# Block-sparse attention feeding a top-1 mixture of experts: five routing groups, unscaled copies of K, early gathers freed from the later scatters, setup moved

## The chip, the cores and the metric

The kernel runs on one core of a Trainium2 chip. The metric is the time of one execution in device microseconds, as the median of three runs. The trace is of one execution of its own. Engines are named as in the profile: PE multiplies matrices, PEld loads its weights, DVE, ACT and POOL are the vector, scalar and GpSimd engines, SP issues direct DMAs. Each engine works through its instructions in the order in which they were written; an instruction that waits holds up everything behind it on the same engine.

## The reference

```python
scores = q @ k.T / sqrt(64)                 # batch 4, heads 8, 768 tokens, 24 blocks of 32
mask: neighbouring blocks, first and last block row and column, 3 sampled blocks per block row
attn = softmax(where(mask, scores, -1e9)) @ v          # -> x of 3072 rows x 512
e_idx = argmax(x @ w_gate)                             # 8 experts, one per row
gate = softmax(x @ w_gate)[e_idx] * sigmoid(x @ w_output_gate)[e_idx]
out = gate * (relu(x @ w1[e_idx]) @ w2[e_idx])         # 512 -> 1024 -> 512
```

All inputs are fp32. The sampled blocks and the routing are data, so K and V blocks are fetched by index at run time and rows of x travel through a table in DRAM that is sorted by expert.

## The kernel before

**Steps of the attention.** The work is written out as steps. Two batch pairs (bp 0 and 1) take 26 steps each: four dense ones for the first and last block row (`Dense`), then 22 sparse ones (`Sparse`): 11 pairs of block rows, each pair in two steps (head groups 0 and 1). Sparse steps of bp 0 are steps 4 to 25, of bp 1 steps 30 to 51. In a step PE writes the scores S (line 507, or 574 in a dense step), DVE takes the row maxima (514, 583), ACT the exponentials P (522, 591); one step later PE transposes P to T (471), ACT and DVE copy it to SBUF; two steps later PE multiplies it with V into O (539, 550, 608), and DVE normalises into a slot of the ring `xall` (483 to 485). S and T each have two PSUM buffers. The program text of step n is: S of n, hooks of rank 0, O of n-2, maxima of n, hooks of rank 1, normalisation of n-2, hooks of rank 2, T of n-1, exponentials of n, hooks of rank 3. Side work is hung on a step and a rank with `at(step, rank, ...)`.

**Feeding a sparse pair.** For pair i with first step u0, POOL copies six sampled blocks of K by index into one of three buffers `kr` (`gather_k`, line 439) at the ends of steps u0-3 and u0-2, DVE copies the four neighbouring blocks (`window_k`, 445 and 446), and POOL fetches the V rows with two indirect DMAs (`gather_v`, 456) in steps u0-1 and u0. Every copy of K multiplies by 1/8. The first and last K block are put into the three buffers once per bp (`fixed`, 415). q of a pair comes by DMA into a ring of four slots, `qall` (`load_q`, 405).

**Routing.** A tile is 128 rows of x; there are 24, twelve per bp. A finished tile is transposed (`turn`, 630; ACT's or DVE's copy to xT is 634 or 636) and multiplied with the gate weights (`route_p`, 646). Tiles are ranked in groups (`RG`): `route_a` (ten DVE instructions), `route_r` (PE products with a triangle and with ones, 689 to 694), `route_b` (two on ACT), `route_c` (seven or eight on DVE), then for each tile one scatter of its rows into the table `rows` in DRAM by POOL (`route_d`, 760), out of its slot of `xall` (tile t has slot t mod NX). All of a group's work hangs on the step in which its last tile is done.

**Early expert.** After group GE, that is after twelve tiles, the fullest expert is chosen (`choose`). 512 rows of it are gathered out of the table (`load_early`, 902, four gathers) and turned (`turn_early`, 913, 917, 918) while attention still runs, so that the experts can begin before all rows are placed. The framework orders an access of `rows` behind earlier ones that it can't tell apart; scatters are declared independent of each other, and the gathers name the scatters that they need.

**Experts.** Behind step 53 the program of the experts is dealt out (`program`): pieces n of 128 hidden columns, eight to a unit of rows. Per piece ACT and DVE split the fp32 weights into two fp16 parts (`w_h` 972, `w_l` 976), PE computes h (`p_h`, 998), ACT and DVE split h (`h_h` 1007, `h_l` 1013), PE computes y four pieces later (`p_y`, 1033). h takes the two PSUM buffers of T. Within a program step, work is sorted by rank. `plan` (0, 1, 2) computes on DVE, with one small product (831), where the remaining rows lie; the gathers of all later units wait for it.

**Start.** PE first runs 66 products on a tile of ones (`warm`), then the dense steps as their K, q and V land.

Of the kernel before, what the change touches and what calls it, by code (L numbers as in the profile page):

```python
# [33 lines left out]
NX = 8  # L34
# [28 lines left out]
RG = ((0, 3), (3, 6), (6, 9), (9, 12), (12, 16), (16, 19), (19, 22), (22, 24))  # L63
GT = max(b - a for a, b in RG)

GE = 3
# [22 lines left out]
XE = 52, 53  # L89
XG = 42, 43, 48, 49  # L90

LATE_T = 52
PARTS = (5, 5, 4), (6, 9)

KC = (("pool", 3, (0, 1, 2)), ("pool", 2, (3, 4, 5)))
NWARM = 66
WARM = {}
# [31 lines left out]
def tile_kernel(ctx, tc, q, k, v, sampled, wg, wcat, out):  # L129
# [39 lines left out]
    xs0 = const.tile([128, 2, 4, EU], F16, name="xs0")  # L169
# [11 lines left out]
    eighth = const.tile([128, 1], F32, name="eighth")  # L181
# [13 lines left out]
    nc.vector.memset(eighth, EXPS)  # L195
# [90 lines left out]
    def setup_vals():  # L286
        nc.vector.tensor_copy(pw, pl["places"])
        nc.vector.tensor_copy(stack[:, 1, 0:8], bins[0:PS])
        nc.vector.tensor_scalar(ckey, bins, -16.0 * LS - 1.0, 8.0, op0=ALU.mult, op1=ALU.add)
# [5 lines left out]
    def setup_index():  # L295
# [4 lines left out]

        vf = sp.tile([128, 2, 12], F32, name="vf")
# [109 lines left out]
    e8th = eighth.unsqueeze(2).to_broadcast([128, 4, 64])  # L411

    def fixed(bp, r):
        for j in range(2):
            nc.gpsimd.tensor_tensor(
                kr[r][:, 10 + j], kn[bp][:, :, 23 * j], e8th, op=ALU.mult)
# [7 lines left out]
    def gather_k(bp, i, kind, ns):  # L424
# [5 lines left out]
        for n, rv in zip(ns, regs):  # L430
            slot = n + 4 if n < 3 else n - 2
            if kind == "dve":
                nc.vector.tensor_single_scalar(
                    r[:, slot], kn[bp][:, :, ds(rv, 1)].rearrange("p u o n -> p u (o n)"), EXPS, op=ALU.mult)
            elif kind == "act":
                nc.scalar.activation(
                    r[:, slot], kn[bp][:, :, ds(rv, 1)].rearrange("p u o n -> p u (o n)"), AF.Copy, scale=EXPS)
            else:
                nc.gpsimd.tensor_tensor(  # L439
                    r[:, slot], kn[bp][:, :, ds(rv, 1)].rearrange("p u o n -> p u (o n)"), e8th, op=ALU.mult)  # L440

    def window_k(bp, i):
        a = 1 + 2 * i
        r = kr[i % RK]
        nc.vector.tensor_single_scalar(r[:, 0], kn[bp][:, :, a + 2], EXPS, op=ALU.mult)
        nc.vector.tensor_single_scalar(
            r[:, 7:10].rearrange("p s u n -> p u s n"), kn[bp][:, :, a - 1:a + 2], EXPS, op=ALU.mult)
# [309 lines left out]
    scattered = []  # L757

    def route_d(t):
# [5 lines left out]
        scattered.append(i.name)  # L765

# [133 lines left out]
    def gather_x(u, x, m):  # L900
        place_ = place_u[:, WALK[u - 1], m:m + 1] if u else place_0[:, m:m + 1]
        after_scatters(nc.gpsimd.indirect_dma_start(  # L902
            x.bitcast(I32), None, rows, bass.IndirectOffsetOnAxis(ap=place_, axis=0)).ins, NT if u else RG[GE][1])

# [201 lines left out]
    for bp in range(2):  # L1106
        o = PER * bp
        for r in range(RK):
            at(o + r, 3, fixed, bp, r)
# [244 lines left out]
```

## Time and profile before

| | us |
|---|---|
| median of three runs (533.68 to 539.52) | 534.85 |
| the profiled execution | 530.91 |
| its span in the trace, first to last instruction | 529.1 |
| PE busy | 494.4 |
| DVE, ACT, POOL busy | 360.6, 299.0, 259.2 |

Attention and routing take about the first 255 us, the experts run from about 245 us to the end. Start times in the timeline are microseconds from the start of the span. A bracket at the end of a line of the timeline is the idle time of that engine just before and what ended it.

### The profile page before, as it was taken

What the parts mean: (1) busy time and instruction counts of PE and PEld (TensorE: products, weight loads), DVE (VectorE), ACT (ScalarE), POOL (GpSimd) and SP (SyncE); (2) the same over time, 40 slices, a digit from 0 to 9 for tenths busy, and PEclk for the clock granted to TensorE, in tenths of its full rate; (3) what the DMA queues carried; (4) which work ended last, traced back from release to release, by engine and by line L of the source; (5) the groups of instructions that cost most, each with busy time, mean ns of one, the idle gap of its engine ahead of it and who ended that gap; (6) DMA issues with size and microseconds to landing.
All of it is one profiled execution on the core that took longest, in us unless ns stands there. A gap on an engine that the chain in (4) does not pass through costs nothing.

```text
span 529.1 us, 18264 instructions
## 1 busy us (share of the span) xinstructions
PE 494.4 (93%) x7363; PEld 335.2 (63%) x7363; DVE 360.6 (68%) x736; ACT 299.0 (57%) x542; POOL 259.2 (49%) x411
## 2 busy tenths in 40 slices
PE   7999999998989998878899999999999999996994
PEld 5666776676767776655345665666566666665653
DVE  2788888766789786848758374655557666568870
ACT  3556666665557566555337554554565646567661
POOL 7797878781578877853150324040503404226222
PEclk9999999999989999999899999999999999997998
DMA  7967889893967778766579999599788988799801
GB/s 294 302 223 222 249 258 287 253 308 105 272 203 245 240 196 257 244 220 217 202 251 365 344 379 336 202 283 263 274 213 311 252 256 312 206 301 329 229 30 38
DMA packets 59903, 131.88 MB, mean 249 GB/s; under 512 B 28320, under 2 KB 28448, under 8 KB 59810
## 3 DMA queue, kind: packets, MB, share of 16 engines
q1 hardware_dynamic: 47314, 86.84, 53.1%
q0 software_dynamic: 12496, 43.79, 24.8%
q8 instruction: 60, 0.98, 0.8%
q14 instruction: 33, 0.27, 0.2%
HBM read 112.06 MB, written 12.85 MB: 236 GB/s over the span
## 4 chain that ended last, share of the span: by engine, by line
PE 57%; POOL 13%; issue 12%; POOLq 6%; DMA 5%; DVE 4%; ACT 1%; ACTq 0%; DVEq 0%
PE y L1033 25%; PE h L998 24%; POOL kr L439 8%; POOLq L428 5%; DMA vt<-in_v_dram,vidx 3%; POOL vt L456 2%; POOL rows L760 1%; DMA wx<-rows,place 1%; PE S L507 1%; PE O L550 1%; PE T L471 1%; PE S0d L574 1%; PE Od L608 1%; DMA raw<-in_sampled_dram 1%; DVE kr L976 1%
## 5 line engine op out<-in xcount | busy, mean ns | idle before, releaser
L976 DVE SCALAR_TENSOR_TENSOR kr<-r,kr 128x1024 f16<-128x1024 f32 x80 | 96.1, 1222 | 30.9 <-ACT kr L972 30.9
L1051 POOL DMA_INDIRECT out_dram<-yo,tab x28 | 33.0, 1178 | 171.1 <-ACT yo L1043 166.5
L1033 PE MATMUL y<-kr,hh 128*128 128x512 f16 (+3 forms) x759 | 110.6, 312 | 0.0
L998 PEld LDWEIGHTS <-kr 128*128 128x128 f16 x960 | 78.6, 98 | 40.9 <-issue 11.4
L1033 PEld LDWEIGHTS <-hh 128*128 128x128 f16 (+3 forms) x984 | 61.3, 98 | 58.2 <-issue 10.9
L998 PE MATMUL h<-xall,kr 128*128 128x256 f16 (+5 forms) x864 | 90.2, 252 | 4.6 <-DVE kr L976 4.6
L1007 ACT ACTIVATE hh<-h 128x512 f16<-128x512 f32 (+5 forms) x64 | 31.6, 494 | 104.7 <-PE h L998 75.6
L439 POOL TENSOR_TENSOR kr<-kn,eighth 128x256 f32<-128x256 f32 x132 | 79.4, 632 | 6.5 <-issue 5.2
L972 ACT ACTIVATE kr<-r 128x1024 f16<-128x1024 f32 x80 | 82.1, 1052 | 0.0
L522 ACT ACTIVATE P<-S,mx 128x256 f32<-128x256 f32 x176 | 69.7, 492 | 9.2 <-DVE mx L514 9.2
L1013 DVE SCALAR_TENSOR_TENSOR hh<-h,hh 128x512 f16<-128x512 f32 (+5 forms) x64 | 35.7, 558 | 51.6 <-ACT hh L1007 51.3
L514 DVE TENSOR_REDUCE mx<-S 128x4 f32<-128x1024 f32 x44 | 53.6, 1218 | 19.7 <-PE S L507 10.6
L456 POOL DMA_INDIRECT vt<-in_v_dram,vidx x44 | 43.6, 990 | 26.3 <-PE O L550 15.7
L507 PE MATMUL S<-kr,qall 64*32 64x256 f32 x1408 | 51.0, 382 | 3.8 <-POOL kr L439 3.3
L474 ACT COPY pt<-T 128x512 f32<-128x512 f32 x66 | 36.6, 593 | 27.5 <-PE T L471 27.5
L471 PE MATMUL T<-ident,P 128*128 128x128 f32 x352 | 47.7, 278 | 0.0
L760 POOL DMA_INDIRECT rows<-xall,place x24 | 25.3, 1056 | 33.0 <-issue 13.0
L471 PEld LDWEIGHTS T<-ident,P 128*128 128x128 f32 x352 | 39.1, 142 | 2.6 <-ACT P L522 0.3
L902 POOL DMA_INDIRECT xb<-rows,place_u x24 | 30.3, 1264 | 16.2 <-DVE place_u L838 9.3
L550 PE MATMUL O<-vt,pt 128*32 128x65 f32 x1408 | 32.0, 225 | 6.5 <-DMA vt<-in_v_dram,vidx 5.4
L1033 PE MATMUL y<-wx,hh 128*128 128x512 f16 (+3 forms) x225 | 36.1, 321 | 0.0
L976 DVE SCALAR_TENSOR_TENSOR wx<-r,wx 128x1024 f16<-128x1024 f32 x24 | 29.0, 1224 | 9.6 <-ACT wx L972 9.6
(273 smaller groups left out, 698.2 us busy)
## 6 DMA issues: line engine op xcount, KB each, us to landing
r<-in_wcat_dram SPq DMA_DIRECT2D x104, 512.0 KB, 4.8
vq<-in_v_dram SPq DMA_DIRECT2D x8, 780.0 KB, 6.6
qall<-in_q_dram SPq DMA_DIRECT2D x24, 256.0 KB, 3.4
vcall<-in_v_dram SPq DMA_DIRECT2D x22, 260.0 KB, 4.6
kn<-in_k_dram SPq DMA_DIRECT2D x10, 384.0 KB, 5.3
kn<-in_k_dram SPq DMA_DIRECT2D x3, 768.0 KB
vcall<-in_v_dram SPq DMA_DIRECT2D x12, 130.0 KB, 6.5
vt<-in_v_dram,vidx POOLq DMA_INDIRECT x44
```

The costliest lines, as they stand in the source:

```text
L439: nc.gpsimd.tensor_tensor(r[:, slot], kn[bp][:, :, ds(rv, 1)].rearrange("p u o n -> p u (o n)"), e8th, op=ALU.mult)
L456: nc.gpsimd.indirect_dma_start(vt[bp, i][:, s].rearrange("p b j w -> p (b j w)"), None, v, bass.IndirectOffsetOnAxis(ap=vidx[:, bp, i, s:s ...
L471: nc.tensor.transpose(pt[:, 128 * c:128 * c + 128], p[:, 128 * c:128 * c + 128], ident)
L474: nc.scalar.copy(t[:, 0:w], pt[:, 0:w])
L507: nc.tensor.matmul(s[64 * b + 32 * qi:64 * b + 32 * qi + 32, h2, hp], t[p, 64 * j + 32 * qi:64 * j + 32 * qi + 32], g[p, 1 - qi:3:1 + qi, ...
L514: nc.vector.tensor_reduce(mx, self.s.rearrange("p b h n -> p (b h) n"), axis=AX.X, op=ALU.max, negate=True)
L522: nc.scalar.activation(p[:, 256 * hp:256 * hp + 256], self.s[:, b, hp], AF.Exp, bias=self.mx[:, 2 * b + hp:2 * b + hp + 1])
L550: nc.tensor.matmul(o[row:row + 32, h2, hp, 0:VW], t[:, col:col + 32], av[:, qi, h2, j], start=False, stop=h2 == 1 and hp == 1)
L972: nc.scalar.activation(w[:, 0, r], piece(n // 8, n % 8)[:, r], AF.Copy, scale=SW)
L976: nc.vector.scalar_tensor_tensor(w[:, 1, r], piece(n // 8, n % 8)[:, r], SW, w[:, 0, r], op0=ALU.mult, op1=ALU.subtract)
L998: nc.tensor.matmul(hps[g][:, cols(n)], w[:, hl, 128 * c:128 * c + 128], x[:, xl, c, 0:t], start=cnt == 0, stop=cnt == 11)
L1033: nc.tensor.matmul(y[t * p:t * p + t, 0:d], a[:, k:k + t], w[:, l, 512 + d * p:512 + d * p + d], start=n % 8 == 0 and cnt == 0, stop=n % 8 ...
```

## The change

The routing groups become 6, 6, 5, 5 and 2 tiles in place of 3, 3, 3, 3, 4, 3, 3 and 2. The early expert is still chosen after twelve tiles, which is now the second group. The ring of finished tiles has twelve slots in place of eight; the memory comes from the turned early rows, which now lie in `qall`. The scatters of the first group are spread over every second step. The early gathers hang on steps 42 to 45 in place of 42, 43, 48 and 49, and depend on the first twelve scatters only; later scatters no longer depend on them. K is copied without a factor, by plain copies, and each pair's q is scaled on ACT at the end of step u0-3 (u0-1 for the first); q is loaded one step earlier. Two thirds of the DVE setup moves from steps 4 and 5 to the start. `fixed` for the second and third buffer of bp 0 moves from steps 1 and 2 to 3 and 4. Sixteen products on ones follow the scores of step 0. In the experts' program, `plan` 0 and 1 come behind the weights of their step, and the split of h of pieces 0 and 1 comes one step earlier. `declare_no_dep(..., keep=...)` is a call of the framework: it drops the dependencies within the group except on the instructions kept.

```diff
-NX = 8
+NX = 12
-RG = ((0, 3), (3, 6), (6, 9), (9, 12), (12, 16), (16, 19), (19, 22), (22, 24))
+RG = ((0, 6), (6, 12), (12, 17), (17, 22), (22, 24))
-GE = 3
+GE = 1
-XE = 52, 53
-XG = 42, 43, 48, 49
+XE = 51, 52
+XG = 42, 43, 44, 45
-PARTS = (5, 5, 4), (6, 9)
+PARTS = (4, 3, 4), (5, 6)
-NWARM = 66
+NWARM, NFILL = 66, 16
-    xs0 = const.tile([128, 2, 4, EU], F16, name="xs0")
...
     def setup_vals():
         nc.vector.tensor_copy(pw, pl["places"])
         nc.vector.tensor_copy(stack[:, 1, 0:8], bins[0:PS])
+
+    def setup_keys():
         nc.vector.tensor_scalar(ckey, bins, -16.0 * LS - 1.0, 8.0, op0=ALU.mult, op1=ALU.add)
...
         nc.vector.tensor_copy(index, pp[0:PS, 0:5])
 
+    def setup_rows():
         vf = sp.tile([128, 2, 12], F32, name="vf")
...
     def fixed(bp, r):
         for j in range(2):
-            nc.gpsimd.tensor_tensor(
-                kr[r][:, 10 + j], kn[bp][:, :, 23 * j], e8th, op=ALU.mult)
+            nc.gpsimd.tensor_copy(kr[r][:, 10 + j], kn[bp][:, :, 23 * j])
...
-                nc.gpsimd.tensor_tensor(
-                    r[:, slot], kn[bp][:, :, ds(rv, 1)].rearrange("p u o n -> p u (o n)"), e8th, op=ALU.mult)
+                nc.gpsimd.tensor_copy(r[:, slot], kn[bp][:, :, ds(rv, 1)].rearrange("p u o n -> p u (o n)"))
...
-        nc.vector.tensor_single_scalar(r[:, 0], kn[bp][:, :, a + 2], EXPS, op=ALU.mult)
-        nc.vector.tensor_single_scalar(
-            r[:, 7:10].rearrange("p s u n -> p u s n"), kn[bp][:, :, a - 1:a + 2], EXPS, op=ALU.mult)
+        nc.vector.tensor_copy(r[:, 0], kn[bp][:, :, a + 2])
+        nc.vector.tensor_copy(r[:, 7:10].rearrange("p s u n -> p u s n"), kn[bp][:, :, a - 1:a + 2])
...
-        after_scatters(nc.gpsimd.indirect_dma_start(
-            x.bitcast(I32), None, rows, bass.IndirectOffsetOnAxis(ap=place_, axis=0)).ins, NT if u else RG[GE][1])
+        n = NT if u else RG[GE][1]
+        i = nc.gpsimd.indirect_dma_start(
+            x.bitcast(I32), None, rows, bass.IndirectOffsetOnAxis(ap=place_, axis=0)).ins
+        after_scatters(i, n)
+        if not u:
+            tc.declare_no_dep(i, group="table", reason="rows of first tiles", keep=kept[:n])
+            tc.add_to_no_dep_group("table", i)
...
-        x = xs[0] = xs0
+        x = xs[0] = qall.rearrange("p r n -> p (r n)").bitcast(F16).rearrange("p (l c t) -> p l c t", l=2, c=4)
...
     setup_const()
+    setup_rows()
+    setup_keys()
...
-            at(o + r, 3, fixed, bp, r)
+            at(o + r if bp or not r else r + 2, 3, fixed, bp, r)
...
-                at(u0 - 5, 1, load_q, bp, i)
+                at(u0 - 6, 1, load_q, bp, i)
+            at(u0 - 3 if bp or i else u0 - 1, 3, scale_q, bp, i)
...
-                        at(t0 + 5 + (t - a), 3, route_d, t)
+                        at(t0 + 5 + (t - a) * (1 if g else 2), 3, route_d, t)
...
-        at(n, 0, turn_early, 2 * m)
+        at(n, 3, turn_early, 2 * m)
...
-            do(PLAN[i], 8.5 if i == 2 else 5, plan, i)
+            do(PLAN[i], 8.5 if i == 2 else 12.5, plan, i)
...
-                do(n + 1, 10, h_h, bank_of(n))
-                do(n + 1, 11, h_l, bank_of(n))
+                do(n + (n > 1), 10 if n > 1 else 16, h_h, bank_of(n))
+                do(n + (n > 1), 11 if n > 1 else 16, h_l, bank_of(n))
...
             now.pS()
+            if step == 0:
+                warm(NFILL)
```

## Rows read from the trace of the kernel before

**Rows 1.** The page: busy time, share of the span and instructions of each engine.

```profile
PE 494.4 (93%) x7363; PEld 335.2 (63%) x7363; DVE 360.6 (68%) x736; ACT 299.0 (57%) x542; POOL 259.2 (49%) x411
```

**Rows 2.** Windows: stretch, length; busy us (instructions) per engine; clock, DMA share, GB/s.

```profile
44.00:119.00 75.00, 71.20 (x1832) 53.92 (x1830) 59.67 (x156) 48.86 (x118) 59.90 (x90) 1.00 0.86 268
204.00:245.00 41.00, 32.81 (x759) 25.05 (x755) 27.34 (x78) 23.61 (x52) 23.89 (x33) 1.00 0.69 225
```

**Rows 3.** Windows of 1 and 2 us with a lowered clock.

```profile
11.00:12.00 1.00, 1.00 (x8) 0.67 (x11) 0.12 (x1) 1.00 (x3) 1.00 (x4) 0.50 1.00 418
258.00:260.00 2.00, 2.00 (x6) 0.68 (x5) 1.86 (x12) 0.00 (x0) 0.00 (x0) 0.50 0.00 0
```

**Rows 4.** Timeline of 0 to 30 us: start, us, engine, line, operation, [idle before].

```profile
1.05 5.28 PE L188 MATMUL warm<-ones 128*128 128x128 f16 x66 [1.05 <-DVE eighth L195]
1.37 0.29 POOL L149 CAST ident<-ident 128x128 f16<-128x128 f32 x1
...
5.93 0.63 ACT L409 ACTIVATE qall<-qall 128x512 f32<-128x512 f32 x1 [3.70 <-DMA qall<-in_q_dram]
...
8.85 0.96 DVE L583 TENSOR_REDUCE mx0d<-S0d 128x1 f32<-128x768 f32 x1 [5.60 <-PE S1d L574]
...
10.56 0.56 PE L471 MATMUL T0d<-ident,P00d 128*128 128x128 f32 x3 [1.77 <-POOL dd L340]
...
14.63 0.96 DVE L583 TENSOR_REDUCE mx0d<-S0d 128x1 f32<-128x768 f32 x1 [2.19 <-PE S0d L574]
```

**Rows 5.** Timeline of 190 to 226 us: steps 42 to 49.

```profile
193.73 0.57 DVE L446 TENSOR_SCALAR kr<-kn 128x768 f32<-128x768 f32 x1
193.85 1.09 PE L507 MATMUL S<-kr,qall 64*32 64x256 f32 x32
...
200.56 0.59 ACT L634 COPY xT<-xp 128x512 f32<-128x512 f32 x1 [1.20 <-PE xp L630]
...
204.99 1.13 PE L507 MATMUL S<-kr,qall 64*32 64x256 f32 x32
...
207.57 1.05 POOL L760 DMA_INDIRECT rows<-xall,place  x1 [2.59 <-DMA wx<-rows,place]
...
216.42 1.08 PE L507 MATMUL S<-kr,qall 64*32 64x256 f32 x28 [1.71 <-POOL kr L439]
```

**Rows 6.** The page's DMA issues: count, KB each, us to landing.

```profile
qall<-in_q_dram SPq DMA_DIRECT2D x24, 256.0 KB, 3.4
```

**Rows 7.** Timeline of 17 to 46 us, the first sparse steps.

```profile
27.71 1.66 PE L507 MATMUL S<-kr,qall 64*32 64x256 f32 x32
...
28.00 0.48 ACT L474 COPY pt0d<-T0d 128x384 f32<-128x384 f32 x1
...
32.01 0.58 DVE L289 TENSOR_SCALAR ckey<-bins 128x8 f32<-128x8 f32 x1
...
39.71 0.18 DVE L323 COPY vals<-vf 128x24 f32<-128x24 f32 x1
...
44.14 1.09 PE L507 MATMUL S<-kr,qall 64*32 64x256 f32 x32
```

**Rows 8.** Timeline of 138 to 157 us: DVE's and POOL's copies of K side by side.

```profile
146.34 2.19 DVE L446 TENSOR_SCALAR kr<-kn 128x768 f32<-128x768 f32 x1
146.35 1.75 POOL L439 TENSOR_TENSOR kr<-kn,eighth 128x256 f32<-128x256 f32 x3
```

**Rows 9.** Timeline of 225 to 265 us: the end of attention.

```profile
230.23 1.09 PE L507 MATMUL S<-kr,qall 64*32 64x256 f32 x32
...
236.68 1.22 DVE L918 SCALAR_TENSOR_TENSOR xs<-xe,xs 128x1024 f16<-128x1024 f32 x1 [1.93 <-ACT xs L917]
237.90 0.66 PE L550 MATMUL O<-vt,pt 128*32 128x65 f32 x30 [2.15 <-DMA vt<-in_v_dram,vidx]
...
256.71 6.99 PE L998 MATMUL h<-xs,kr 128*128 128x512 f16 x24 [2.53 <-DVE hh L1013]
...
263.63 0.19 PE L831 MATMUL lb<-left,ones 21*128 21x42 f16 x1
```

More of the change, by code (lines that the diff above doesn't have):

```diff
@@ L88 @@
 XT = {1: 6}
-XE = 52, 53
-XG = 42, 43, 48, 49
+XE = 51, 52
+XG = 42, 43, 44, 45
 LATE_T = 52
-PARTS = (5, 5, 4), (6, 9)
+PARTS = (4, 3, 4), (5, 6)
 KC = (("pool", 3, (0, 1, 2)), ("pool", 2, (3, 4, 5)))
-NWARM = 66
-WARM = {}
+NWARM, NFILL = 66, 16
 def in_order(tc):
@@ L180, in tile_kernel @@
     sw128 = const.tile([128, 1], F32, name="sw128")
-    eighth = const.tile([128, 1], F32, name="eighth")
     zero = const.tile([128, 1], F32, name="zero")
@@ L194, in tile_kernel @@
     nc.vector.memset(sw128, SW)
-    nc.vector.memset(eighth, EXPS)
     raw = const.tile([128, NB * 3, 2], I32, tag="raw", name="raw")
@@ L409, in scale_q @@
         nc.scalar.activation(qt[bp, i], qt[bp, i], AF.Copy, scale=EXPS)
-    e8th = eighth.unsqueeze(2).to_broadcast([128, 4, 64])
     def fixed(bp, r):
         for j in range(2):
-            nc.gpsimd.tensor_tensor(
-                kr[r][:, 10 + j], kn[bp][:, :, 23 * j], e8th, op=ALU.mult)
+            nc.gpsimd.tensor_copy(kr[r][:, 10 + j], kn[bp][:, :, 23 * j])
     def fixed_v(bp, r):
@@ L432, in gather_k @@
             if kind == "dve":
-                nc.vector.tensor_single_scalar(
-                    r[:, slot], kn[bp][:, :, ds(rv, 1)].rearrange("p u o n -> p u (o n)"), EXPS, op=ALU.mult)
+                nc.vector.tensor_copy(r[:, slot], kn[bp][:, :, ds(rv, 1)].rearrange("p u o n -> p u (o n)"))
             elif kind == "act":
-                nc.scalar.activation(
-                    r[:, slot], kn[bp][:, :, ds(rv, 1)].rearrange("p u o n -> p u (o n)"), AF.Copy, scale=EXPS)
-            else:
-                nc.gpsimd.tensor_tensor(
-                    r[:, slot], kn[bp][:, :, ds(rv, 1)].rearrange("p u o n -> p u (o n)"), e8th, op=ALU.mult)
+                nc.scalar.copy(r[:, slot], kn[bp][:, :, ds(rv, 1)].rearrange("p u o n -> p u (o n)"))
+            else:
+                nc.gpsimd.tensor_copy(r[:, slot], kn[bp][:, :, ds(rv, 1)].rearrange("p u o n -> p u (o n)"))
     def window_k(bp, i):
@@ L444, in window_k @@
         r = kr[i % RK]
-        nc.vector.tensor_single_scalar(r[:, 0], kn[bp][:, :, a + 2], EXPS, op=ALU.mult)
-        nc.vector.tensor_single_scalar(
-            r[:, 7:10].rearrange("p s u n -> p u s n"), kn[bp][:, :, a - 1:a + 2], EXPS, op=ALU.mult)
+        nc.vector.tensor_copy(r[:, 0], kn[bp][:, :, a + 2])
+        nc.vector.tensor_copy(r[:, 7:10].rearrange("p s u n -> p u s n"), kn[bp][:, :, a - 1:a + 2])
     def window_v(bp, i):
@@ L755, in part @@
             next(gens[f, g], None)
-    scattered = []
+    scattered, kept = [], []
     def route_d(t):
@@ L765, in route_d @@
         scattered.append(i.name)
+        kept.append(i)
     def after_scatters(i, n):
```

## Prediction

> **What bounds the kernel now.** I first read the busy shares: PE is busy for 494.4 of 529.1 us, no other engine for more than 360.6 [rows 1]. So PE is the engine to gain from, and the question is where it stands idle or slow. The windows answer where. From 44 to 119 us, most of the sparse steps of bp 0, PE is busy for 71.20 of 75 us; from 204 to 245 us, the last sparse steps and the change to the experts, for 32.81 of 41 us: 8.2 us idle in a twelfth of the span [rows 2]. In neither stretch is another engine full: POOL has 59.90 of 75 and 23.89 of 41 us. The windows also show the clock: it is at 0.50, the lower of its two levels (1.2 in place of 2.4 GHz), just after PE's first pause and again at 258 us after another pause [rows 3]. Then I read the timeline at each pause, for what ended it. From about 265 us on, through the experts, PE has next to no pause that the change touches, so I take that part as it is, only earlier or later.
>
> **The change, part by part.** The times go against the profiled execution, 530.91 us.
>
> *Scaled q, plain copies of K.* 22 scalings of q go to ACT, 0.63 us each by the one that exists [rows 4], 13.9 us in all. They run after the exponentials of an odd step, where ACT next waits for the transposed tile, 1.20 us idle before its copy at 200.56 [rows 5]: 0.63 fits in, so I take 0 for 19 of them. Without that cover each would cost 0.63. Their DMA is no wait either: 3.4 us from issue to landing [rows 6] against some three steps of 3.7 us. The first two pairs are different: both scalings stand behind the exponentials of step 3, and S of step 4 (27.71) and ACT's copy at 28.00 [rows 7] are queued behind them, 0.6 to 1.3 us, which I set against the gain of the setup below; the second pair of bp 1 meets such a copy too, 0 to 0.6 us, set against the next point.
>
> POOL's 132 copies drop the factor. The trace has no plain copy of 128x256 on POOL. The bounds are the multiplication with a second input, 1.75 us for three or 0.58 each [rows 8], and the plain cast of half as many columns, 0.29 [rows 4]. Such a cast also pays what an instruction costs at all, so I take 0.40: 0.18 saved per copy, about 1.1 us per pair of steps. The Trainium skill ("GPSIMD Engine Reference", section 3.1) says that two inputs share one read port, at about 2.6 cycles an element against 1.0 to 1.8 with one input; that would be an estimated 0.25 to 0.4 us, in which case the gain is as I take it or larger.
>
> DVE's copies keep their size, but they lose time beside POOL's: `window_k` took 2.19 us while three POOL copies ran for 1.75 [rows 8], and 0.57 without them [rows 5]. It ended 0.4 us after the train of three, not after the first of them. The Trainium skill ("SBUF — State Buffer", Who interferes with whom) says that the two engines hold a shared port for one whole instruction and the other waits for it; by that the wait would be at most one copy, about 0.6 us, and the change worth nothing here. The row says the whole train, so a train shorter by 0.55 us releases S at the start of bp 1 earlier by as much; with the scaling there, I take 0 (from -0.6 to 0.6).
>
> *Early gathers and the larger ring.* In steps 46 to 50 POOL waits in its queue: the scatter at 207.57 stood 2.59 us for an early gather to land [rows 5]. Behind it stand the V gathers and the K copies of the next pairs, and PE waits for those: 1.71 us at 216.42 [rows 5]. A step without such waits is 3.71 us: from S at 193.85 to S at 204.99 are three steps in 11.14 us [rows 5]. From 204.99 to 230.23 [rows 9] are five in 25.24, where 18.57 would do: 6.7 us too much. After the change POOL has nine indirect DMAs in the nine steps 42 to 50, at about 1.3 us with the issue, plus two V gathers and six copies per pair: 2.6 + 2.6 + 2.4 + 0.3 = 7.9 us in 7.4. It loses 0.5 us per pair, 2 us over four pairs, against a lead of about a step. So the waits go nearly all: I take 6.0 us; at least the 2.6 of the one wait, at most 6.7. What is late next is DVE, below.
>
> *Setup.* 24 small DVE instructions, first and last at 32.01 and 39.71 [rows 7] and at about 0.2 us each 4.9 us, run before the first maxima instead, where DVE is idle for 5.60 us [rows 4]. From S at 27.71 to S at 44.14 are four steps in 16.43 [rows 7], 1.6 more than four full ones, and the first of them has no O of a sparse step yet, so more is to be had. I take 2.0 after the two scalings: at least 0.3 (1.6 - 1.3), at most 4.3 (4.9 - 0.6). If the cover at the start failed, the 4.9 us would come in front of the first maxima.
>
> *Sixteen products on ones.* 66 took 5.28 us [rows 4], so sixteen take 1.28, and PE's pause before 10.56 is 1.77 [rows 4]: they fit. After the pause the clock is low [rows 3] and the second maxima begin at 14.63 [rows 4]. At the full clock the 3.6 us from 11 to 14.63 would take half, 1.8 less; but part of them is PE waiting for the exponentials of step 0. I take 1.2; at least 0, where the clock falls all the same, at most 1.8.
>
> *Five groups.* Ranking takes n(n+3)/2 products for n tiles: 73 before, 99 after. 26 more, each below the 0.08 us of a 128-column product [rows 4]: 0 to 2.1 us, I take 0.7, as they have 8 columns. In return some 54 instructions leave DVE and six leave ACT, with the stalls of two rankings of bp 0. PE's 3.8 us of idle time from 44 to 119 [rows 2] come from these and from POOL; I take 2.0 back (0 to 3.8).
>
> *The end of attention.* The wait of 2.15 us for V before 237.90 [rows 9] goes, but most of it isn't gained: DVE is at the early rows (236.68 to 237.90) just then, and from there to the last plan instruction DVE has hardly a gap. The wait of 2.53 us before 256.71 [rows 9] is for the split of h, which stood behind twelve plan instructions. It now stands in front of them, but the split of piece 2 stands behind them, and PE's fifth h needs it. Adding up DVE's queue in its new order from the rows' durations (1.2 per split of weights, 0.7 per split of h, 2.5 and 1.7 for the two parts of the plan), the plan ends some 2 us later in DVE's order, and PE comes to the small product, now at 263.63 [rows 9], 2.2 us earlier, if the clock doesn't fall for longer. I take 1.8 (0 to 4).
>
> *What else moves.* The DMA of q now shares a step with the V window on SP's queue, two issues in one step and none in the next: 0. The second pair of early gathers passes four scatters on POOL's queue; that is counted in the nine above. The early rows in `qall` must wait for the last read of q, S of step 51, which is in front of their products on PE anyway: 0. The second turn of early rows passes the gate product of tile 22 on PE, and the first weights on ACT and DVE, which have the same work in another order: within the 1.8. `fixed` of bp 0 clears POOL's way for the first pair's K and comes back two steps later: within the 2.0. Five scatters in place of three at step 53 take POOL 2.6 us longer, but it has nothing else to do until the plan is out behind 263.63 [rows 9]: 0; without that cover the next unit's gathers would be 2.6 us later.
>
> The sum: 6.0 + 2.0 + 1.2 + 2.0 + 1.8 - 0.7 = 12.3 us. 530.91 becomes 518.6. The median of the runs lies 3.9 us over the profiled execution, and I put the same on top: 534.85 - 12.3 = 522.5.
>
> **The rivals.** *POOL stays late.* Copies that cost 0.55, or a DVE that holds them up [rows 8], make 9 us of POOL work in 7.4 per pair; the lead is gone after two pairs and the stalls of steps 46 to 50 come back by half. Gain 12.3 - 3 - 2 = 7: 527.5. For it speaks that POOL is at 0.80 without gathers [rows 2], against it that the 2.59 of plain waiting can't come back.
>
> *DVE takes it over.* If the end of attention gains nothing, the clock falls in the first pause and the setup gives only its lower bound, 12.3 - 1.8 - 1.2 - 1.7 = 7.6 remain: 527. All three hang on DVE or the clock and not on POOL.
>
> *No change.* The gathers still hold up POOL, because the DMA itself is late and not the dependency: 6.0 becomes about 1, and the plain copies bring nothing: 530 to 533. Against it: the wait before 207.57 names the gather, which the change takes out.
>
> *Slower.* Now ACT waits for q, in order. Should q land later than three steps after its issue, 11 us, every pair would hold up ACT's copies of T and with them PE. At 1 us each, 22 pairs cost 22 us, and 534.85 - 12.3 + 22 = 544.5. It decides where a q DMA takes over 11 us; 3.4 is the median [rows 6], so only a queue of weights or V in front of it could do that.
>
> **How the numbers follow.** The forecast (gain 8 to 18, 517 to 527) has 0.55, POOL late 0.14, DVE 0.13, no change 0.10, slower 0.08. The predicted time is the forecast's, 522.5. The range goes down to 515 (6.7 + 4.3 + 1.8 + 3.8 + 4 = 20.6, not all at once) and up to 531, which takes in POOL and DVE late and part of no change. A measurement of this kernel tells about 1% from no change, 5.3 us: below 529.5 is faster. That is the forecast, DVE, most of POOL late, 0.76; within 1% 0.16; slower 0.08.
>
> **What the profile after would show.** Right: no scatter of POOL waits for a gather; five steps from S of step 46 to S of step 51 in under 20 us; POOL's copy at about 0.4 us; ACT's scaling in a former idle stretch; clock 1.0 at 11 us; steps 5 to 8 at 3.7 to 3.9 us; the small product of the plan about 12 us earlier than 263.63, and the experts as long as before. Wrong: ACT waiting for qall in every pair; POOL's copies at 0.55; PE waiting longer than 2.5 us for DVE at the first h; the experts longer than before, because weights come later than PE now wants them.

## The result and the profile after

| | before | after |
|---|---|---|
| median of the runs | 534.26 us (532.47 to 539.52, four runs) | 524.84 us (523.38 to 525.99, four runs) |
| ratio, 95% interval | | 0.9858, 0.9814 to 0.9902 |
| the profiled execution, its span | 530.91, 529.1 | 523.96, 522.2 |

The change gains 9.4 us between the medians and 6.95 us between the two profiled executions, on the chip of these runs. The experiments ran in three further sets, each on one chip with its own runs of the kernel before. The kernel before took 532.96, 544.88 and 544.05 us there; the changed kernel, which ran in the last two sets again, took 531.40 and 531.58 us (ratios 0.9697, 0.9625 to 0.9769, and 0.9780, 0.9730 to 0.9829). I call these sets two, three and four, and the runs of the table set one. Between kernels of different sets only the ratios can be compared, and these only roughly: the ratio of the same two kernels lies between 0.9697 and 0.9858 in the three sets that have both. Set two has no run of the changed kernel as it is. Nearest to it there is the changed kernel with two scalings of q moved, 524.38 us, ratio 0.9798 (0.9723 to 0.9874).

The page's busy times of the changed kernel, beside [rows 1]:

```profile
PE 495.4 (95%) x7405; PEld 336.4 (64%) x7405; DVE 347.8 (67%) x683; ACT 309.5 (59%) x558; POOL 227.9 (44%) x411
```

PE does as much work as before in 6.9 us less; POOL is 31 us lighter, ACT 10.5 us heavier. The windows of the changed kernel (columns as in [rows 2]):

```profile
44.00:119.00 75.00, 71.30 (x1799) 54.52 (x1798) 51.74 (x126) 51.05 (x121) 44.98 (x90) 0.98 0.81 264
204.00:245.00 41.00, 37.03 (x789) 26.88 (x788) 27.56 (x68) 25.70 (x54) 21.03 (x32) 0.96 0.76 250
11.00:12.00 1.00, 0.70 (x7) 0.39 (x8) 0.56 (x1) 1.00 (x3) 1.00 (x4) 1.00 1.01 424
117.00:119.00 2.00, 2.00 (x35) 1.83 (x25) 0.77 (x3) 0.09 (x1) 1.28 (x4) 0.50 0.60 241
240.00:242.00 2.00, 2.00 (x6) 0.73 (x5) 2.00 (x3) 0.01 (x1) 1.70 (x1) 0.50 1.01 360
```

The first window is the disappointment: DVE has 8 us less to do there, POOL 15 us, and PE is idle for 3.7 us as before (3.8 in [rows 2]). The second is the success: 4.0 us idle in place of 8.2. The third shows the full clock at 11 us, where [rows 3] has 0.50; but the next two show stretches at 0.50 at 117 and at 240 us. The kernel before has such stretches at 151 and at 257 us too. Now the timeline of the changed kernel at the places of [rows 4, 5, 7 to 9]. The program's line 499 is S (507 before), 531 and 542 are O, 996 is h, 824 the small product of the plan:

```profile
8.60 1.07 PE L185 MATMUL warm<-ones 128*128 128x128 f16 x16
10.43 0.52 PE L463 MATMUL T0d<-ident,P00d 128*128 128x128 f32 x3 [0.77 <-ACT P00d L583]
...
13.50 0.96 DVE L575 TENSOR_REDUCE mx0d<-S0d 128x1 f32<-128x768 f32 x1 [1.54 <-PE S0d L566]
...
27.30 1.15 ACT L408 ACTIVATE qall<-qall 128x512 f32<-128x512 f32 x2
28.07 1.10 PE L499 MATMUL S<-kr,qall 64*32 64x256 f32 x32 [1.18 <-ACT qall L408]
...
91.12 0.66 PE L499 MATMUL S<-kr,qall 64*32 64x256 f32 x13 [0.89 <-issue]
...
116.68 1.09 PE L542 MATMUL O<-vt,pt 128*32 128x65 f32 x30 [1.17 <-DMA vt<-in_v_dram,vidx]
...
145.05 1.51 POOL L433 COPY kr<-kn 128x256 f32 x3
145.21 0.76 DVE L439 COPY kr<-kn 128x768 f32<-128x768 f32 x1
...
204.41 1.09 PE L499 MATMUL S<-kr,qall 64*32 64x256 f32 x32
...
210.12 1.00 POOL L752 DMA_INDIRECT rows<-xall,place  x1 [0.17 <-issue]
210.33 0.81 PE L499 MATMUL S<-kr,qall 64*32 64x256 f32 x17 [1.31 <-issue]
...
225.15 1.09 PE L499 MATMUL S<-kr,qall 64*32 64x256 f32 x32
...
254.09 2.75 PE L996 MATMUL h<-qall,kr 128*128 128x512 f16 x12 [1.72 <-DVE hh L1011]
256.86 0.19 PE L824 MATMUL lb<-left,ones 21*128 21x42 f16 x1
```

The products on ones are over at 9.67 us and PE's pause behind them is 0.77 us. S of step 4 waits 1.18 us for the two scalings of q. The scatter at 210.12, which is the one of 207.57 in [rows 5], waits for no gather; the five steps from S of step 46 (204.41) to S of step 51 (225.15) take 20.74 us in place of 25.24. The plan's small product runs 6.8 us earlier than in [rows 9], not 12.

Three rows of the page complete the picture: POOL's plain copy, the landing of q, and the queue that brings PE its instructions (packets, MB, share of 16 engines).

```profile
L433 POOL COPY kr<-kn 128x256 f32 x132 | 48.5, 407 | 9.1 <-issue 7.8
...
qall<-in_q_dram SPq DMA_DIRECT2D x24, 256.0 KB, 4.7
...
q8 instruction: 60, 0.98, 0.8%
```

**Where the pauses went.** I summed all pauses of PE's products over 0.15 us from 26 us to 262 us by what the timeline names as their end:

| pauses of PE, us | all | V | K | split of h | ACT's exponentials | ACT's scaling | nothing shown ("issue") |
|---|---|---|---|---|---|---|---|
| before, set one | 18.91 | 5.41 | 3.28 | 2.53 | 3.35 | - | 1.65 |
| after, set one | 13.05 | 2.33 | 0 | 1.72 | 0.58 | 1.19 | 5.24 |
| before, set three | 20.59 | 0.81 | 2.18 | (2.53, past 262 us) | 3.02 | - | 10.10 |
| after, set three | 15.17 | 0.91 | 0 | 1.71 | 0.54 | 1.18 | 7.90 |

The waits at which the change aimed are down from 14.57 (V, K, h, exponentials) to 4.63 us in set one. That is some 10 us, close to what I had added up. 3.6 us of it came back as pauses that end for nothing the profile shows, and 1.2 us as the wait for the scaling.

### The profile page after: what moved, and what is told of

It reads as the page before. It is cut to its first block, busy times and chain, and to the rows that moved or that the text cites. A ratio compares the mean times of both kernels' runs of the same rounds, so it can differ in the third digit from the quotient of the medians.

```text
span 522.2 us, 18317 instructions
## 1 busy us (share of the span) xinstructions
PE 495.4 (95%) x7405; PEld 336.4 (64%) x7405; DVE 347.8 (67%) x683; ACT 309.5 (59%) x558; POOL 227.9 (44%) x411
## 4 chain that ended last, share of the span: by engine, by line
PE 70%; issue 9%; DMA 7%; POOL 6%; POOLq 3%; DVE 2%; ACT 0%; SPq 0%; ACTq 0%; DVEq 0%
PE y L1031 24%; PE h L996 24%; PE S L499 6%; PE T L463 5%; PE O L542 4%; PE O L531 3%; DMA vt<-in_v_dram,vidx 3%; POOLq L424 3%; DMA xall<-vcall 3%; POOL kr L433 2%; PE xp L622 2%; PE lp L638 2%; DMA vq<-in_v_dram 1%; DMA raw<-in_sampled_dram 1%; DVE kr L974 1%
## 5 line engine op out<-in xcount | busy, mean ns | idle before, releaser
L433 POOL COPY kr<-kn 128x256 f32 x132 | 48.5, 407 | 9.1 <-issue 7.8
L996 PE MATMUL h<-xall,wx 128*128 128x256 f16 (+4 forms) x288 | 36.1, 277 | 0.0
```

The source lines that it names most:

```text
L433: nc.gpsimd.tensor_copy(r[:, slot], kn[bp][:, :, ds(rv, 1)].rearrange("p u o n -> p u (o n)"))
L996: nc.tensor.matmul(hps[g][:, cols(n)], w[:, hl, 128 * c:128 * c + 128], x[:, xl, c, 0:t], start=cnt == 0, stop=cnt == 11)
```

## Experiments

**One part undone (set two).** First the early gathers, back in their steps and ordered against later scatters:

```diff
-XG = 42, 43, 44, 45
+XG = 42, 43, 48, 49
-        if not u:
-            tc.declare_no_dep(i, group="table", reason="rows of first tiles", keep=kept[:n])
-            tc.add_to_no_dep_group("table", i)
```

> The changed kernel with only the early gathers put back: steps 42, 43, 48 and 49, and later scatters ordered behind them again. Own theory (the dependency held POOL up, and PE behind it): the stretch from S of step 46 to S of step 51 grows from 20.74 us to some 25 us, and a scatter of POOL waits over 2 us for an early gather; the time is 524.84 + 4.5 = 529.3 us (the prediction's term of 6.0 would give 530.8). Rival (POOL's load in these steps, not the dependency, makes the waits): the stretch stays within 1 us of 20.74 and the time at 525.

Measured: 529.40 us (ten runs), ratio 0.9934 (0.9893 to 0.9975), against 0.9858 for the whole change in set one. From its timeline:

```profile
219.71 0.99 POOL L895 DMA_INDIRECT wx<-rows,place  x1 [4.79 <-DMA rows<-xall,place]
...
229.53 0.97 POOL L895 DMA_INDIRECT wx<-rows,place  x1 [4.96 <-DMA rows<-xall,place]
230.81 0.95 POOL L448 DMA_INDIRECT vt<-in_v_dram,vidx  x1 [0.30 <-issue]
...
235.58 0.66 PE L542 MATMUL O<-vt,pt 128*32 128x65 f32 x16 [9.08 <-DMA vt<-in_v_dram,vidx]
```

The old gathers hold POOL up, but not where and not quite as the theory has it. The gathers wait 4.79 and 4.96 us in POOL's queue for the scatters ahead of them, the V gather stands behind them until 230.81, and PE waits 9.08 us for its rows; a scatter waits 1.63 us for a gather at most. And this is behind step 51. The stretch from step 46 to step 51 was 19.9 us by the maxima (201.66 to 221.53), not 25: there the rival's figure came true. Beside the nearest kernel of its own set the time is 5.0 us worse (529.40 against 524.38, and the intervals of the two ratios don't overlap), and the small product of the plan comes 5.8 us later (261.10 against 255.30). So the old gathers are a real cost, near the 4.5 expected. The edit puts back their steps and the dependency together, so it doesn't say which of the two costs it. The speed of steps 46 to 51 isn't owed to their removal alone: with them back, POOL was early enough there all the same. That its shorter copies gave it that lead is my reading, and the run with scaled copies, below, speaks against it as the only reason: with long copies and freed gathers the four steps from the maxima of step 46 to those of step 50 take 16.6 us, against 15.6 here, 17.1 with the whole change and 19.8 before. In this stretch either part seems to be enough.

The routing groups:

```diff
-RG = ((0, 6), (6, 12), (12, 17), (17, 22), (22, 24))
+RG = ((0, 3), (3, 6), (6, 9), (9, 12), (12, 16), (16, 19), (19, 22), (22, 24))
-GE = 1
+GE = 3
-PARTS = (4, 3, 4), (5, 6)
+PARTS = (5, 5, 4), (6, 9)
```

> The changed kernel with only the eight routing groups put back (3, 3, 3, 3, 4, 3, 3, 2, with the scatters of a group in successive steps). The prediction's terms (2.0 for the instructions saved, 0.7 lost on PE): 524.84 + 1.3 = 526.1 us, lost between 44 and 119 us. Own theory now, from the changed kernel's trace, where steps 9 to 25 gained only 0.4 us: these steps are bound by PE, so eight groups cost nothing there: 524 to 525.5. Rival (the five big groups bunch their DVE work, as at step 43 and 44, 4.36 and 4.28 us long): eight groups are faster, 523 or less, and steps 43 and 44 take under 4 us.

Measured: 528.66 us (four runs), ratio 0.9892 (0.9795 to 0.9989): too wide to choose by. Its pauses tell more. Between 44 and 119 us not one ends on DVE, with eight groups as with five; the kernel before had 0.89 us of these. So in the changed kernel the regrouping takes nothing off PE in this stretch that a pause shows, and the 2.0 us that I had given it were not there to take. Steps 42 to 45 took 15.7 us from maxima to maxima against 15.8, so the big groups cost nothing either.

The copies of K (the diff shows POOL's sampled blocks; `fixed` and DVE's `window_k` get their factor back too):

```diff
-            at(u0 - 3 if bp or i else u0 - 1, 3, scale_q, bp, i)
...
-                nc.gpsimd.tensor_copy(r[:, slot], ...)
+                nc.gpsimd.tensor_tensor(r[:, slot], ..., e8th, op=ALU.mult)
```

> The changed kernel with only the factor 1/8 put back into the copies of K (POOL multiplies, about 0.6 us each in place of 0.41) and the scalings of the pairs' q taken out. Theory of the prediction (POOL is late without the plain copies): stalls of PE for kr come back in steps 33 to 50, 3 to 5 us, less the 1.2 us that the two first scalings cost: 526.6 to 528.6 us. Rival (the copies had room enough, and the scalings only cost): S of step 4 starts at about 26.6 in place of 28.07 us, no new wait for kr, time 523.4 us.

Measured: 532.70 us (ten runs), ratio 0.9955 (0.9905 to 1.0006), that is within its interval no better than the kernel before, with the gathers freed and the rest of the change in place. Its timeline and its group of copies:

```profile
26.48 1.09 PE L503 MATMUL S<-kr,qall 64*32 64x256 f32 x32
...
34.85 1.08 PE L503 MATMUL S<-kr,qall 64*32 64x256 f32 x28 [1.88 <-POOL kr L437]
...
L437 POOL TENSOR_TENSOR kr<-kn,eighth 128x256 f32<-128x256 f32 x132 | 78.8, 625 | 6.3 <-issue 4.4 <-POOL xall L627 1.0
```

Both halves of both theories show. S of step 4 starts 1.6 us earlier without the scalings, and two steps later PE waits 1.88 us for POOL, whose copies take 0.625 us again; waits for K come to 3.0 us in all (this trace is of an execution of 536.22 us, so a long stretch of it says little). The whole cost is over the 2 to 4 expected: some 5 us if the ratio is set against that of set one, 8.3 us against the nearest kernel of its own set (532.70 against 524.38; the intervals of the ratios don't overlap, and neither of the two waits for a scaling at step 4). It is as large as what the rival "POOL stays late" had, 3 + 2, but not in the same place: the rival's 2 are stalls of steps 46 to 50, and these don't come back (16.6 us, above). The copies are a large part of this change, not a side matter.

The first two scalings, moved to where ACT was idle:

```diff
-            at(u0 - 3 if bp or i else u0 - 1, 3, scale_q, bp, i)
+            at(*((u0 - 3, 3) if bp or i > 1 else (3 + i, i)), scale_q, bp, i)
```

> The changed kernel with only the first two scalings of q moved: that of pair 0 ahead of ACT's copy of the third tile of step 2, that of pair 1 ahead of the exponentials of step 4, where ACT stands idle for 1.77 and 1.52 us. Own theory (the two scalings in front of S of step 4 cost what PE waits there, 1.19 us, and all steps up to 25 are bound by PE): S of step 4 starts at about 26.9 us in place of 28.07, S of step 25 is still 1 us early, and the time is 523.6 us. Rival (the time is given back at the next waits, for the exponentials of step 5 at 35.61 and for V): S of step 25 where it was, 524.8 us.

Measured: 524.38 us (four runs), ratio 0.9798 (0.9723 to 0.9874). S of step 4 starts at 26.77 with no wait, and the plan's small product is at 255.30 in place of 256.86. (This trace is of an execution of 531.48 us, with one pause of 5.76 us far behind, at 306 us.) The interval of its ratio overlaps that of the change in set one; set four takes this up.

**The same two kernels once more (set three).**

> The kernel before once more, for a second trace of it. In its first trace PE stood still for 18.91 us between 26 and 262 us (pauses over 0.15 us), of which V 5.41, K 3.28 and pauses that end for nothing the profile shows (issue) 1.65. Own theory (these sums belong to the kernel): V 4 to 7, K 2.5 to 4, issue 1 to 3 us. Rival (they belong to the single execution): sums that are off by more than half.

> The changed kernel once more, for a second trace of it. In its first trace PE's pauses between 26 and 262 us sum to 13.05 us: issue 5.24, V 2.33, ACT's scaling of q 1.19. Own theory (the change has put issue pauses in the place of others): issue 4 to 6.5 us again, at least twice that of the kernel before. Rival (chance of one execution): issue under 3 us.

Measured: 549.31 us (ten runs) and 531.40 us (four). For the kernel before this is a ratio of 1.0044 (0.9993 to 1.0094) to the other runs of the same kernel in this set, 544.88 us: two medians of one kernel on one chip lie 4.4 us apart, as much as a large term of the prediction. Both of my theories on the pauses were wrong. Issue pauses are 10.10 us before and 7.90 after (table above), so they are no product of the change: on this chip the kernel before has more of them. Only on the first chip did they come in place of other waits. The kernel before at step 4 and at the plan's product:

```profile
28.40 1.09 PE L507 MATMUL S<-kr,qall 64*32 64x256 f32 x28 [1.16 <-POOL kr L439]
...
272.61 0.19 PE L831 MATMUL lb<-left,ones 21*128 21x42 f16 x1
```

and in the changed kernel:

```profile
260.56 0.19 PE L824 MATMUL lb<-left,ones 21*128 21x42 f16 x1
```

That is a lead of 12.05 us, where set one has 6.77. (The trace of the kernel before is of an execution of 549.07 us, 4.2 over the 544.88, so this pair shows a larger gain, 17.5 us, than the medians of the set, 13.5.) And the kernel before keeps its clock at the start here without any products on ones; a window and the maxima of step 1:

```profile
11.00:14.00 3.00, 2.91 (x26) 1.59 (x25) 1.02 (x2) 1.30 (x3) 2.88 (x14) 1.00 1.02 427
...
13.54 0.96 DVE L583 TENSOR_REDUCE mx0d<-S0d 128x1 f32<-128x768 f32 x1 [1.36 <-PE S0d L574]
```

**The load of q (set three).** The changed kernel with the load one step later, and the kernel before with it one step earlier:

```diff
-                at(u0 - 6, 1, load_q, bp, i)
+                at(u0 - 5, 1, load_q, bp, i)
```

> The changed kernel with only the load of q put back by one step (five steps ahead of its use in place of six), so that it no longer shares a step with the V window, and in bp 0 with a part of the next K. Own theory (three transfers of 256 to 384 KB next to the two V gathers delay the 16 KB packets of PE's instructions and the V rows, and PE then pauses): issue pauses between 26 and 262 us fall from 5.24 to under 3 us, the time to 521.5 to 523. Rival (the bunching is harmless, which the prediction took, with 0 for it): issue pauses as before, time within 1 us of 524.8.

> The kernel before with only the load of q moved one step earlier, as the change does it, so that it shares a step with the V window. Own theory (the bunched transfers delay PE's instructions and V): issue and V pauses between 26 and 262 us grow from 1.65 and 5.41 by 2 to 4 us together, time 1 to 4 us above the kernel before. Rival (harmless): sums and time as in the kernel before.

Measured: 529.90 us, ratio 0.9653 (0.9579 to 0.9728), beside 0.9697 for the change in the same set: not to be told apart. Issue pauses 6.98 against 7.90 us. The other way round 543.72 us, ratio 0.9957 (0.9919 to 0.9996): not slower, though issue and V pauses sum to 12.98 against 10.91 us. By the times the rival holds, and the 0 that I gave the load of q stands. The sum of the pauses went the theory's way by 2.1 us, but that is one trace of each kernel.

**Set four: clock, scalings, load of the queues.**

> The changed kernel unchanged, as the one to compare the next three with on their chip. Two pairs of traces so far gave a lead over the kernel before at the plan's small product of 6.8 us (256.86 against 263.63) and of 12.1 us (260.56 against 272.61). Own theory: the ratio to the kernel before lies between the two measured, 0.970 and 0.986; pauses of PE that end for nothing the profile shows (issue) sum to 5 to 8 us between 26 and 262 us. Rival (the first pair was the odd one): ratio at 0.97 or lower.

Measured: 531.58 us (six runs), ratio 0.9780 (0.9730 to 0.9829): between the two, as the theory has it; issue pauses 7.70 us.

Both edits from above together, the first two scalings and the load of q:

> The changed kernel with two edits: the first two scalings of q moved to where ACT stood idle (ahead of the copy of the third tile of step 2, and ahead of the exponentials of step 4), and the load of q five steps ahead of its use in place of six. Own theory (the two scalings cost PE 1.19 us in front of S of step 4, and that is kept to the end; the load of q is worth little): 1.2 to 2.5 us faster than the changed kernel on this chip, S of step 4 at about 26.8 us. Rival (later waits take it back): within 0.7 us of it.

Measured: 529.13 us (six runs), ratio 0.9752 (0.9694 to 0.9810), 2.45 us under the change in the median, with intervals that overlap. Its timeline:

```profile
22.25 0.63 ACT L408 ACTIVATE qall<-qall 128x512 f32<-128x512 f32 x1
...
26.85 1.09 PE L499 MATMUL S<-kr,qall 64*32 64x256 f32 x32
...
28.89 0.64 ACT L408 ACTIVATE qall<-qall 128x512 f32<-128x512 f32 x1
```

Both scalings now stand in idle time of ACT, and S of step 4 waits for nothing. The lead over the unchanged kernel of this set, by the maxima, is 1.0 us at step 5, 1.4 at step 19 and 2.9 at step 25; it isn't taken back. It is the best version that I have, though a measurement doesn't separate it from the change.

Without the products on ones:

```diff
-NWARM, NFILL = 66, 16
+NWARM, NFILL = 66, 0
```

> The changed kernel without the sixteen products on ones behind the scores of step 0. The prediction's term: the clock falls to 0.5 after PE's first pause, and step 2 starts 1.2 us later (first maxima of step 1 at 14.6 in place of 13.5). Rival (the second trace of the kernel before kept the clock at 1.0 there without such products, its first maxima of step 1 at 13.54): clock 1.0 at 11 us, maxima at 13.5, and no difference in time.

Measured: 532.48 us (six runs), ratio 0.9804 (0.9757 to 0.9851), 0.9 us over the change and not to be told from it. A window and the maxima of step 1:

```profile
11.80:15.20 3.40, 3.40 (x19) 1.99 (x19) 0.71 (x2) 0.27 (x1) 3.13 (x18) 0.50 1.02 426
...
14.64 0.96 DVE L575 TENSOR_REDUCE mx0d<-S0d 128x1 f32<-128x768 f32 x1 [2.69 <-PE S0d L566]
```

Here the theory's step is right: the clock is at 0.50 and step 1 is 1.42 us late (14.64 against 13.22 in the unchanged kernel of this set). But at step 20 only 0.3 us of it are left (91.22 against 90.95). Between the maxima of steps 19 and 20 the unchanged kernel loses 1.5 us, at this pause, which the kernel without the products doesn't have there (it has others, of 0.69 us at 76.71 for one):

```profile
90.14 0.66 PE L499 MATMUL S<-kr,qall 64*32 64x256 f32 x13 [0.89 <-issue]
```

Last, the load of the DMA queues:

```diff
     def load_q(bp, i):
...
+        if i < NPAIR and (bp or i > 2):
+            return
...
     def window_v(bp, i):
+        if bp or i > 2:
+            return
```

> The changed kernel without the loads of q and of the V window from the fourth pair of bp 0 on (about 0.5 of 2 MB per pair; the scores and the routing are computed on old data, so only the steps of attention are to be read). Own theory (full DMA queues delay PE's instructions and the V rows): pauses that end for nothing the profile shows between 44 and 232 us fall below a third of those of the changed kernel on this chip, and V pauses with them. Rival (these pauses do not depend on the load of the DMA queues): they stay within a third.

Measured, between 44 and 232 us: issue pauses 6.00 us against 7.70, V pauses 0 against 2.25. (The time, 670 us, says nothing: other routing means other experts.) By their sum the issue pauses don't depend on the load: the rival's third holds. The sum mixes two kinds of pauses, though, which the next part takes apart. That the V pauses hang on the load fits their 0, but it is one trace, and in the other traces of this set they are 0.60 and 0.78 us with the full load.

**What an issue pause is.** The trace also records the packets that bring PE's instructions, 16 KB each, 40 of them between 26 and 262 us. In the changed kernel of set one, all eight issue pauses end 1.3 to 1.7 us after such a packet has landed:

| packet landed, us | 59.09 | 83.69 | 89.71 | 145.81 | 156.78 | 192.63 | 208.81 | 229.92 |
|---|---|---|---|---|---|---|---|---|
| PE goes on | 60.56 | 85.03 | 91.12 | 147.47 | 158.24 | 194.17 | 210.33 | 231.38 |
| between | 1.47 | 1.34 | 1.41 | 1.66 | 1.46 | 1.54 | 1.52 | 1.46 |

The packet behind the pause at 91.12 can be followed through the variants, whose PE program is the same at this place. In the changed kernel of three sets, and with the old gathers, it started at 87.7 to 88.8 us, and PE paused by 0.6 to 0.9 us. In five variants it started 100 to 210 PE instructions earlier in the program, and there was no pause: scalings moved (alone and with the load of q), q loaded a step later, no products on ones, q and V window left out.

The place in the program says it more sharply than the time. The trace has 15004 records of PE (products, loads of weights and those of its sequencer) to 60 packets, 250 to a packet. Counted from the start, the eight pauses of the table end at records 2241, 3521, 3777, 6081, 6593, 8385, 9153 and 10177: all of them 193 beyond a multiple of 256. So do three of the four of the kernel before in set one and all 21 of the four kernels of set two. So these pauses are waits for a late packet, and which packet is late changes with small shifts of the rest. The Trainium skill ("Runtime: NRT & Kernel Launch", Instruction fetch mechanics) describes this queue: blocks of 256 instructions, fetched while the current one executes, at a cost that is mostly hidden. Here it isn't: 5.24 us in the attention of the changed kernel in set one.

In sets three and four most issue pauses are of another kind, about 0.4 us long, often two 0.74 us apart with four products between them, and at the same places of the program in each kernel. From the unchanged kernel of set four:

```profile
111.17 0.30 PE L638 MATMUL lp<-wst,xT 128*64 128x16 f32 x4 [0.20 <-issue]
111.91 0.25 PE L638 MATMUL lp<-wst,xT 128*64 128x16 f32 x2 [0.43 <-issue]
...
112.65 0.70 PE L531 MATMUL O<-vcall,pt 128*64 128x65 f32 x15 [0.43 <-issue]
```

and of set three:

```profile
112.37 0.31 PE L638 MATMUL lp<-wst,xT 128*64 128x16 f32 x4 [0.42 <-issue]
113.11 0.71 PE L531 MATMUL O<-vcall,pt 128*64 128x65 f32 x16 [0.43 <-issue]
```

In the unchanged kernel of set four 14 of the 19 issue pauses don't follow a packet in the way of the table, and 15, with 5.88 us, don't end at the place of a packet in the program; four do, with 1.81 us. With the loads of q and V left out (192 in place of 241 GB/s between 44 and 232 us) 12 of the 14 are still there, and no pause over 0.2 us is left that ends at the place of a packet. So the late packets may well hang on the load of the queues, by this one trace; the other kind doesn't. It belongs to the chips of sets three and four: in sets one and two one issue pause of 33 is not at the place of a packet (0.48 us at 34.69 in the kernel before). What it is stays open.

## Why the prediction was right, and where it was not

The time, 524.84 us, is 2.3 us over the predicted 522.5 and well inside the range. The working behind it was less good than the number. I set the lead of the changed kernel, read at the maxima of each step and at the plan's product, beside my terms:

| stretch | term | set one | set three |
|---|---|---|---|
| start to step 2 (products on ones) | 1.2 | 1.13 | 0.16 |
| steps 2 to 9 (setup, less two scalings) | 2.0 | 0.92 | 2.56 |
| steps 9 to 25 (five groups) | 2.0 | 0.43 | 0.79 |
| steps 25 to 33 (start of bp 1) | 0 | 0.08 | 2.61 |
| steps 33 to 46 | 0 | -1.73 | -2.17 |
| steps 46 to 51 (gathers) | 6.0 | 4.25 | 6.58 |
| step 51 to the plan's product | 1.8 | 1.69 | 1.52 |
| from there to the end | 0 | 0.13 | 5.45 |
| rank products, spread | -0.7 | in the above | in the above |
| sum | 12.3 | 6.9 | 17.5 |

**Products on ones.** Right where the clock falls; in set three it doesn't fall at the start of the kernel before, and there is nothing to win. The term is a price times a chance, and I had only the price.

**Setup and scalings.** The mechanism and the place are right: 1.18 us at S of step 4, inside my 0.6 to 1.3. Steps 7 and 8 took 3.73 and 3.91 us from S to S, as I had said of steps 5 to 8, but steps 5 and 6 took 4.04 and 4.66. In set three the kernel before waited 1.16 us for POOL at step 4, and the stretch gained 2.6 us. No run undid the setup by itself, so its share of these numbers isn't shown. The 19 other scalings cost nothing visible, as forecast: no pause of PE names them, although q landed in 4.7 us in place of 3.4.

**Five groups.** This is the step that failed. I took PE's idle 3.8 us in [rows 2] as stalls on DVE and POOL, and half of them as the groups', without adding up what those pauses end on: 0.89 us on DVE, none on POOL's K, 0.98 on issue, 0.72 on V and 0.66 on the exponentials. After the change the stretch has none on DVE, but 1.82 us on issue and 1.53 on V. With eight groups put back, none of the pauses on DVE returned. The saved 54 DVE instructions lay beside other work.

**K copies.** 0.407 us measured, 0.40 taken; the estimate from the Trainium skill ("GPSIMD Engine Reference", section 3.1), 0.25 to 0.4, ends at the measurement. But I gave this part 0 of its own and left its worth inside the term of the gathers. Undone, it costs 5 to 8 us. That the rival "POOL stays late" has a similar price, 5, is partly luck: its stalls of steps 46 to 50 didn't come back.

**Gathers.** No scatter waits for a gather any more, as forecast; the five steps take 20.74 us, where I had put "under 20". The 6.0 came to 4.25. I had read it off the length of the steps; the pauses of PE between 205 and 231 us before sum to 4.46 us (V 2.54, K 1.92). All of these are gone, and one of 1.31 us for PE's own instructions, at 210.33, has come. Behind the stretch, from 226 to 262 us, PE waits 3.42 us for DVE in four pauses and 0.96 for its instructions: there DVE is late next, as I had said.

**Start of bp 1.** I had put 0 (-0.6 to 0.6); set three has 2.61. The 0.08 of set one hides a loss and a gain. 2.15 us are lost from step 25 to 26, where PE waits 1.17 us for V (116.68) and then runs at the clock of 0.50. 2.23 are won from 26 to 33: the kernel before waits there 1.38 us for exponentials and 1.06 for K, the changed kernel for neither. With the scaled copies back, a wait for K of 0.36 us is there again (149.94).

**Steps 33 to 46.** A loss of about 2 us in both sets, for which I had no term but 0.7. With the old gathers these steps took 51.6 us in place of 52.1 (50.4 before), so the early gathers that moved in make up half a microsecond, as far as two sets can be compared. Pauses over 0.15 us make 1.0 of the 1.73 us in set one (1.53 us of issue and V, against 0.49 before) and 1.3 of the 2.17 in set three. The rest isn't settled; my 0.7 for the rank products would fit, but no run shows it by itself.

**The end.** 1.69 and 1.52 for 1.8: the wait of 2.53 us for the split of h is 1.72 now, and V no longer comes late; the order worked out from DVE's queue held. The experts took as long as before in set one (0.13 us). In set three they took 5.45 us less. PE's pauses over 0.15 us behind the plan's product sum there to 10.19 us before and 5.54 after (4.63 and 3.56 in set one); the largest, 5.17 us at 323.09, ends on DVE's split of a later unit's rows. Why that one came late isn't settled. The trace is that of the execution of 549.07 us, and the kernel before has no such pause in set one, so I don't count it for the change.

**The offset.** I carried the 3.9 us by which the median of before lay over its profiled execution to the forecast. The changed kernel's median lies 0.9 over its own. So a sum that was 5.3 us too large in set one met an offset that was 3 us smaller than the one I carried over: the number was saved by the spread of the runs, which is luck. By the medians of sets three and four, 13.5 and 12.5 us, the sum of 12.3 would have been near; by the traces of set three, 17.5, too small.

**The rivals.** "Slower" never came near: q landed in 4.7 us in the median, and no pause but the one at step 4 names it. "No change" falls with the scatter's wait, which is gone. "DVE takes it over" names three terms that fell short; one did (setup), the other two held. None of the rivals named PE's instructions.

## What to carry to other kernels

Before crediting a part with idle time, sum the pauses of the bounding engine in that stretch by what ends each; a saving on another engine is worth little more than the pauses that name it. When waits are removed from an engine that is 95% busy, look at what it waits for next on its own account, its instructions included. And run both kernels on more than one chip before reading a gain of 1 to 3%: the same pair gave 1.4%, 2.2% and 3.0% here, and one kernel against itself on one chip 0.4%.

## What the hardware showed beside this

- **The chip.** The kernel before took 533 to 534 us in two sets and 544 to 545 us in two others (549 when measured a second time in one of them); the changed kernel 525 in set one and 531.5 in the latter two.
- **Instructions of PE.** Late packets of 16 KB stop PE for 0.2 to 1.3 us each, eight times from 26 to 262 us in the changed kernel of set one; which ones are late changes from variant to variant.
- **Copies side by side.** In the kernel before, DVE's copy took 2.19 us beside a train of three on POOL, and POOL lost nothing [rows 8]. Now, with plain copies on both, DVE's took 0.76 and POOL's three 1.51 us (0.62 and 1.07 by themselves): the loss is smaller and mostly POOL's. The rule that I had cited from the Trainium skill ("SBUF — State Buffer", Who interferes with whom), a lock for one instruction, which the page states for DVE's two-port modes, would allow the 0.14 and 0.44 us lost here, but not the 1.62 us that DVE lost before.
- **The clock.** It fell in other places in nearly every execution: at 11, 151 and 257 us before, at 117 and 240 us after in set one, at 227 and 244 us after in set four, with PE pauses of 1 us just ahead of some of them and as long pauses elsewhere (28.07) that left it alone.
